# Attention on 64x64 TensorE tiles, with a range of queries for each half of a key tile

## The chip, the core and the metric

One NeuronCore of a Trainium2 chip runs the whole program. The metric is the time of one execution on the device in microseconds (us); lower is better. "Before" and "changed" are the two kernels. TensorE is PE in the profile (PEld: its weight loads), VectorE is DVE, ScalarE is ACT, GpSimd is POOL, SyncE is SP. "Line" numbers such as L274 differ between kernels, because their source lines differ.

## The reference

Sliding-window attention with a few global keys feeds a balanced mixture of experts. Shapes: batch 4, 8 heads, 768 positions, head size 64; 8 global keys, a window of 96.

```python
scores = (q @ k.T) / 8 - slope[h] * dist          # dist = query - key, or 96 for global keys
keep   = (key < 8) | (0 <= query - key < 96)
a      = softmax(where(keep, scores, -1e9))
x      = a @ v                                     # (3072, 512)
logits = x @ w_gate                                # tokens go to 8 experts, 384 each, best first
out[m] = relu(x[m] @ w1[e]) @ w2[e]                # per expert
```

All of attention is done in fp32, because a small error in a logit sends a token to another expert.

## The kernel before

The program has three parts: a loop over 16 pairs of heads (attention), a routing part that is a chain of short steps, and the experts. A key tile has 120 keys and the 8 global ones; it sees 215 queries. Scores have the keys on partitions, so exp (ACT) and the multiplication with a weight table (DVE) act on `P[128 keys, 2 heads, queries]`.

```python
# scores: 64 rows (head t) x 128 columns (keys); the two heads run side by side
nc.tensor.matmul(ps[:, t, o : o + w], lhsT=kA[r, i, :], rhs=qTt[r, KT * i : KT * i + w], ...)
# attend: 128 rows (keys) x 64 columns (head size)
nc.tensor.matmul(po[n][bk][64 * t : 64 * t + 64, ...], lhsT=v7[:, t, i, :], rhs=P[:, t, ...], ...)
# sums: softmax sums and gate logits, 128 rows x 32 columns, four quarters of the queries side by side
nc.tensor.matmul(pr[32 * gq : 32 * gq + 32, ...], lhsT=onesx[:, t, :], rhs=Ps[n, g][:, t, ...], ...)
...
# one pair, in the order of PE (abridged):
# scores 0 | kT of the next pair | attend of the last group before | scores 1 | qT | attend | sums | scores 2 | tok | attend
# POOL issues 1.5 weight pieces (512 KB each in bf16) per pair: 24 pieces for the experts
```

The softmax here doesn't subtract the row's maximum and nothing guards it: scores larger than these inputs give would overflow.

## Time and profile before

Median 342.42 us (342.17 to 342.49, 3 runs). The parts in the table are of the profiled execution, which took 347.1 us.

| part | from the profile |
|---|---|
| loop over pairs | first scores at 10.6 us, logits complete at 174.1 us: 163 us |
| one pair | 10.0 us |
| routing until the first expert matmul | 68 us |
| experts | 103 us |

Each row of the next view, the table of stretches, gives one stretch of 10 us: its length, the busy time of PE, PEld, DVE, ACT and POOL (with counts), the granted clock, the DMA share and GB/s.

```profile
44.00:54.00 10.00, 10.00 (x142) 7.73 (x140) 6.69 (x13) 4.50 (x8) 4.36 (x6) 1.00 1.07 221
84.00:94.00 10.00, 10.00 (x142) 7.73 (x140) 6.70 (x12) 4.51 (x8) 4.35 (x6) 1.00 1.06 205
94.00:104.00 10.00, 10.00 (x142) 7.74 (x140) 8.03 (x13) 4.51 (x8) 3.31 (x5) 1.00 1.10 255
```

PE is never idle from 24 to 154 us; the next busiest engine, DVE, has 6.0 to 8.1 us of every 10. One pair in the timeline of PE (start, length, engine, line, operation, tiles, shape of one, count):

```profile
80.26 0.87 PE L242 MATMUL pt<-ident,kn 128*128 128x128 f32 x6
81.06 0.98 PE L316 MATMUL po<-P,v 128*64 128x215 f32 x12
81.97 1.00 PE L274 MATMUL ps<-qT,kA 64*128 64x215 f32 x8
82.90 0.87 PE L259 MATMUL pt<-ident,qn 128*128 128x128 f32 x6
83.70 0.95 PE L316 MATMUL po<-P,v 128*64 128x215 f32 x8
84.58 1.63 PE L347 MATMUL pr<-P,onesx 128*32 128x192 f32 x45
...
90.27 0.87 PE L242 MATMUL pt<-ident,kn 128*128 128x128 f32 x6
```

The same step comes again after 10.0 us. The shape of the tile (128*128, 128*64, 64*128, 128*32) changes ten times per pair. The second is q8, a DMA queue that the page calls "instruction":

```profile
PE 275.4 (80%) x2820; PEld 188.1 (54%) x2828; DVE 183.3 (53%) x419; ACT 111.4 (32%) x192; POOL 116.7 (34%) x166
...
q8 instruction: 24, 0.39, 0.4%
```

### The profile page before, as it was taken

How to read it: one execution, taken by the hardware profiler on the slowest of the kernel's cores; microseconds unless marked ns; L12 is line 12 of the kernel's file. 1: busy time of each engine (PE TensorE's matmuls, PEld its weight loads, DVE VectorE, ACT ScalarE, POOL GpSimd, SP SyncE). 2: the span in 40 equal slices, each digit the busy share in tenths (PEclk: the TensorE clock that was granted, in tenths of full speed). 3: DMA queues.
4: the chain of work that ended last, by engine and by line, in shares of the span. 5: the costliest groups of instructions: out<-in, count | busy, mean ns of one | idle time of the engine just before them, and what ended most of it. 6: DMA issues, size and time to landing. Idle time of an engine off the chain costs nothing. (4 is left out here: it accounts for less than half of the span.)

```text
span 345.4 us, 7041 instructions
## 1 busy us (share of the span) xinstructions
PE 275.4 (80%) x2820; PEld 188.1 (54%) x2828; DVE 183.3 (53%) x419; ACT 111.4 (32%) x192; POOL 116.7 (34%) x166
## 2 busy tenths in 40 slices
PE   2899999999999999999923222252969999999990
PEld 2577877777777777777712111131525555555540
DVE  5356768676686667765476666691022233222320
ACT  1575444445534444454200000000314422343220
POOL 8553233535323353530210000006753465223321
PEclk9999999999999999999965555555889999999996
DMA  8999999997999979769099900002322332122111
GB/s 149 250 275 219 232 220 229 214 240 197 220 260 190 271 167 215 155 124 180 4 167 227 181 3 0 0 1 63 106 91 77 123 129 84 64 91 93 61 63 67
DMA packets 58359, 49.24 MB, mean 143 GB/s; under 512 B 32976, under 2 KB 51920, under 8 KB 58320
## 3 DMA queue, kind: packets, MB, share of 16 engines
q0 software_dynamic: 15808, 26.22, 37.2%
q1 hardware_dynamic: 42512, 22.50, 26.8%
q8 instruction: 24, 0.39, 0.4%
q14 instruction: 15, 0.12, 0.1%
HBM read 56.05 MB, written 9.44 MB: 190 GB/s over the span
## 5 line engine op out<-in xcount | busy, mean ns | idle before, releaser
L282 ACT ACTIVATE P<-ps 128x860 f32<-128x860 f32 (+1 forms) x48 | 42.7, 889 | 64.3 <-PE ps L274 64.3
L794 ACT ACTIVATE hT<-ph 128x384 bf16<-128x384 f32 x64 | 30.9, 490 | 75.8 <-PE ph L791 70.1
L274 PE MATMUL ps<-qT,kA 64*128 64x215 f32 (+2 forms) x448 | 50.7, 352 | 1.5 <-ACT qT L263 1.5
L774 POOL DMA_INDIRECT xe<-x_tok,idi x24 | 23.0, 958 | 80.1 <-DVE idi L631 60.6
L316 PE MATMUL po<-P,v 128*64 128x215 f32 (+6 forms) x576 | 47.5, 298 | 1.0 <-DVE P L296 1.0
L254 POOL COPY kA<-kA 128x56 f32<-128x56 f32 x16 | 16.3, 1017 | 84.0 <-PE po L316 77.5
L791 PE MATMUL ph<-xT,w_all 128*128 128x384 bf16 x256 | 44.4, 332 | 0.2 <-issue 0.2
L274 PEld LDWEIGHTS ps<-qT,kA 64*128 64x128 f32 x448 | 37.6, 191 | 12.1 <-issue 11.0
L316 PEld LDWEIGHTS po<-P,v 128*64 128x64 f32 x576 | 31.4, 136 | 11.8 <-issue 7.4
L289 DVE TENSOR_TENSOR P<-P,Wm 128x860 f32<-128x860 f32 x16 | 28.5, 1784 | 15.4 <-ACT P L282 15.4
L804 POOL DMA_INDIRECT out_dram<-ot,idi x24 | 23.5, 979 | 37.4 <-DVE ot L803 34.2
L791 PEld LDWEIGHTS <-w_all 128*128 128x128 bf16 x256 | 25.5, 100 | 18.5 <-issue 1.6
L296 DVE TENSOR_TENSOR P<-P,Wm 128x860 f32<-128x860 f32 (+1 forms) x32 | 33.6, 1049 | 2.8 <-ACT P L282 2.8
L781 DVE COPY xT<-pxe 128x512 bf16<-128x512 bf16 x24 | 9.6, 422 | 47.0 <-PE pxe L780 35.5
L803 DVE COPY ot<-po 128x512 f32<-128x512 f32 x24 | 16.6, 692 | 29.9 <-PE po L800 27.8
L800 PEld LDWEIGHTS <-hT 128*128 128x128 bf16 x192 | 18.5, 100 | 24.0 <-ACT hT L794 3.4
L347 PEld LDWEIGHTS pr<-P,onesx 128*32 128x32 f32 x768 | 24.7, 109 | 6.0 <-ACT qT L263 4.4
L347 PE MATMUL pr<-P,onesx 128*32 128x168 f32 (+11 forms) x768 | 27.6, 259 | 0.0
L247 DVE COPY kA<-pt 128x360 f32<-128x360 f32 x32 | 17.0, 533 | 15.8 <-PE pt L242 15.8
L800 PE MATMUL po<-w_early,hT 128*128 128x512 bf16 x92 | 23.2, 401 | 2.8 <-ACT hT L794 2.8
L321 ACT COPY oT<-po 128x384 f32<-128x384 f32 x32 | 15.3, 478 | 20.7 <-PE po L316 20.7
L800 PE MATMUL po<-w_late,hT 128*128 128x512 bf16 x92 | 21.2, 379 | 0.1
(145 smaller groups left out, 308.1 us busy)
## 6 DMA issues: line engine op xcount, KB each, us to landing
w_all<-in_moe_w_dram POOLq DMA_DIRECT2D x16, 512.0 KB
v<-in_v_dram SPq DMA_DIRECT2D x32, 180.0 KB, 4.6
kr<-in_k_dram SPq DMA_DIRECT2D x15, 384.0 KB, 7.0
qr<-in_q_dram SPq DMA_DIRECT2D x15, 384.0 KB, 7.3
w_early<-in_moe_w_dram POOLq DMA_DIRECT2D x8, 512.0 KB
w_late<-in_moe_w_dram POOLq DMA_DIRECT2D x4, 1024.0 KB
x_tok<-x SPq DMA_DIRECT2D x16, 192.0 KB, 3.7
v<-in_v_dram SPq DMA_DIRECT2D x32, 14.0 KB
```

The lines of the kernel that those rows point to most:

```text
L247: nc.vector.tensor_copy(out=kA[:, 0 : NT - 1, 8:128].rearrange("c i (u j) -> c i u j", j=NBLK)[:, :, :, 3 * hf : 3 * hf + 3], in_=pt[:, :, ...
L274: nc.tensor.matmul(ps[:, t, o : o + w], lhsT=kA[r, i, :], rhs=qTt[r, KT * i : KT * i + w], start=True, stop=True)
L282: nc.scalar.activation(P[:, :, 0 : GW[g]], ps[:, :, 0 : GW[g]], AF.Exp, scale=0.125)
L289: nc.vector.tensor_tensor(out=P[:, :, 0:430].rearrange("p t (o w) -> p t o w", o=2), in0=P[:, :, 0:430].rearrange("p t (o w) -> p t o w", ...
L296: nc.vector.tensor_tensor(out=P[:, :, 0 : GW[g]], in0=P[:, :, 0 : GW[g]], in1=Wm[:, h0 : h0 + 2, lo : lo + GW[g]], op=ALU.mult)
L316: nc.tensor.matmul(po[n][bk][64 * t : 64 * t + 64, a - QB * bk : z - QB * bk], lhsT=v7[:, t, i, :], rhs=P[:, t, o + a - q0 : o + z - q0], ...
L347: nc.tensor.matmul(o_, lhsT=l_, rhs=r_, start=first[gq], stop=True, skip_group_check=True)
L774: nc.gpsimd.indirect_dma_start(out=xe, out_offset=None, in_=x_tok[:, :], in_offset=bass.IndirectOffsetOnAxis(ap=idi[:, s : s + 1], axis=0),)
L791: nc.tensor.matmul(ph, lhsT=w1_all[:, e, kc, 128 * fc : 128 * fc + 128], rhs=xT_e[:, kc, :, :].rearrange("p t n -> p (t n)"), start=(kc == ...
L794: nc.scalar.activation(hT[:, fc, :], ph, AF.Relu)
L800: nc.tensor.matmul(po, lhsT=hT[:, fc, 128 * t : 128 * t + 128], rhs=w2_of(e)[:, fc, :], start=(fc == 0), stop=(fc == NFC - 1))
L804: s = nc.gpsimd.indirect_dma_start(out=out[:, :], out_offset=bass.IndirectOffsetOnAxis(ap=idi[:, TSLAB * e + t : TSLAB * e + t + 1], axis= ...
```

## The change

The intent: a half of a key tile (64 keys) sees only 151 or 159 queries, not 215. With 64x64 tiles each half gets its own range, and four tiles work at once: two row groups (halves of the keys, or heads) and two column groups. That cuts the streamed columns by a fifth to a quarter (the prediction has the counts). By choice two row groups never write one output bank at the same time, so attend runs in two phases: row group 0 on bank 0 and 1 on bank 1, then swapped, with an ordering dependency between. There are two score groups per pair in place of three; scores and attend now share one tile shape. The token step comes one pair later, one key eviction moves to ACT, one output copy to DVE, and one weight piece is issued per pair.

```diff
-QW = 215
+QW = 159
...
-            for i in GROUPS[g]:
-                for t in range(2):
-                    nc.tensor.matmul(ps[:, t, o : o + w], lhsT=kA[r, i, :], rhs=qTt[r, KT * i : KT * i + w], ...)
+            for i, q0, o, w in PIECES[g]:
+                for c in range(2):
+                    qa = q0 + (56 * c if i < NT - 1 else 0)
+                    for t in range(2):
+                        nc.tensor.matmul(ps[64 * c : 64 * c + 64, t, o : o + w], lhsT=kA[r, i, 64 * c : 64 * c + 64],
+                                         rhs=qTt[r, qa : qa + w], start=True, stop=True, skip_group_check=True)
...
+            for rg in range(2):                    # attend(n, ph): row groups on two banks in turn
+                bk = rg ^ ph
+                lists.append([(rg, bk) + w for w in windows(rg, QB * bk, QB * bk + QB)])
...
+                            mm = nc.tensor.matmul(po[n][bk][64 * t : 64 * t + 64, ...],
+                                                  lhsT=v7[r, t, i, :], rhs=Ps[n, g][r, t, off : off + z - a], ...)
+                            if ph == 1 and m == 0:
+                                tc.add_manual_dep(mm.ins, between[0].ins.name, SYNC_DEP, ...)
...
+                        nc.tensor.matmul(pr[rg][32 * gq : 32 * gq + 32, a:z], lhsT=l_, rhs=r_, ...)   # sums, 64x32 tiles
```

## The prediction

> **What bounds it.** The attention loop runs from 10.6 us (first scores) to 172 us (last sums); the engine table by stretches shows PE 10.00 us busy of every 10 us from 24 to 154 us, granted clock 1.00, DVE 6.7 to 8.1, ACT 4.5, POOL 3.3 to 4.4. The timeline repeats every 10.0 us per head pair. Routing (172 to 233 us, a DVE/PE latency chain) and experts (233 to 345 us) are untouched. So attention is PE bound.

> **One pair's 10.0 us on PE, from the timeline.** Each fp32 matmul is two records of 0.84 ns per column (215 columns: starts 181 ns apart); tiles of one group run concurrently (starts 7 ns apart). Scores 1291 columns per tile, 2.7 us with weight loads; attend 2.5 us; sums 1.9 us (round-robin over tiles of unequal width: a tile idles about 0.2 us[...]); 18 transposes at 109 ns, 2.0 us. Ten changes of tile shape: about 0.09 us empty each, plus a weight load not hidden (50 to 105 ns). [...](last 191-column record should stream out at 89.25, next shape starts at 89.34).

> **The change.**
> - Columns per tile: scores 1291 to 1002, attend 1291 to about 985, sums 668 to about 540, plus 192 for gates as before.
> - Tile-shape changes: 10 to 4 per pair (scores and attend share 64x64). Weight load of 64 columns is 50 ns where it was 105.
> - More records: 138 to 254 per pair. At 7 ns apart when nothing blocks, issue is no limit, but round-robin blocking stays: attend's second phase pairs 127/151/151 with 159/159/88.
> - Replaying these lists[...]: scores 2.0, attend 2.1, sums 1.7, transposes 2.0, changes 0.4: 8.2 us per pair (the same replay gives 10.1 for before).
> - DVE: masks 2 x 1.2 us for 1.05+1.05+1.85, one key eviction (0.7) to ACT, one oT copy (0.55) from ACT, one more transpose and an add (0.6): about 6.5 us. ACT about 4.4. Neither binds at 8.2.
> - Single score buffer, later token step, order wait of attend's second phase: in my replay all answered early in steady state; the first two pairs (W building on ACT) and the longer drain (attend and sums of pair 15 after the last scores) cost about 4 us over 16 x 8.2.
> - Weight pieces: 1 per pair, not 1.5; six move behind the loop. Queue idle in routing (199 to 233 us) absorbs about 20 us.

> **Critical path.** All PE savings are on it until DVE: 16 x 1.8 = 29 us, less about 6 for fill, drain and the longer Dm building on POOL: 22 us.

> **Prediction: 320 us, range 311 to 332. Faster by over 2%: 0.88; within 2%: 0.08; slower: 0.04.**

> **Right if:** timeline period about 8.2 us; PE still over 95% busy in the loop; last sums near 150 us; routing and experts as long as before; DVE about 80% busy; weights landed before the first gather.

> **Wrong if:** four 64x64 tiles don't stream concurrently at 0.84 ns per column (column starts slower than 181/215 of their width: up to 335 us); short windows are bound by weight loads or by dispatch (sums longer than 1.9 us); chains expo-mask-attend or oT-gates stall PE with the single score buffer (PE idle, released by DVE/ACT); late weights delay experts' gathers; or, better, dispatch blocks less than replayed (7.6 us period, 311 us).

10.0 - 8.2 = 1.8 us per pair, 16 x 1.8 = 29 us, less about 6 us: 22 us off 342 us gives 320 us. The 8.2 us are the estimate; its replay gave 10.1 us for the 10.0 us measured before. What the trace of before shows of its terms: records of 215 columns of one tile start 181 ns apart (86.856 and 87.037 us), and the first ones of two tiles 7 ns apart (86.570 and 86.577). The second records of a group come later than that by 105 ns in scores (weights of 128 columns: 286 ns in place of 181) and by 52 ns in attend (64 columns: 233 ns). At a change of shape PE stood empty for an estimated 0.09 us: the last 191-column record starts at 89.088 us, so at 0.84 ns per column it ends at 89.25, and the first record of the next shape starts at 89.342. In sums one tile stood without a record for about 0.2 us: its last 23-column record started at 84.706 us, its next one (143 columns) at 84.938, 6 ns after the third 192-column record of another tile.

## The result, and the profile after

The changed kernel is slower: median 372.19 us (370.07 to 375.11, 4 runs) against 342.46 us, ratio 1.087 (95% interval 1.079 to 1.096). A ratio here is the mean time of one kernel's fast runs over that of the other's in the same rounds, so it is not quite the ratio of the medians quoted. Executions over 1.5% slower than the fastest of the same kernel are left out of the means. The result is correct. The table is of the profiled executions, 347.1 us before and 375.1 us changed.

| | before | changed | predicted |
|---|---|---|---|
| loop over pairs | 163 us | 193 us | about 140 us |
| routing | 68 us | 69 us | as before |
| experts | 103 us | 100 us | as before |

All of the loss is in the loop. The table of stretches of the changed kernel, with the same columns as before:

```profile
44.00:54.00 10.00, 8.15 (x235) 7.10 (x236) 5.73 (x12) 3.12 (x7) 3.38 (x4) 1.00 0.77 167
84.00:94.00 10.00, 5.84 (x77) 5.38 (x74) 1.96 (x7) 1.60 (x3) 0.00 (x0) 0.66 0.55 93
94.00:104.00 10.00, 10.00 (x300) 9.19 (x300) 7.94 (x16) 5.12 (x9) 4.15 (x5) 1.00 0.64 140
```

PE now idles for part of the time, and every other engine idles more: none took over as the limit. The third stretch is fully busy and holds 300 records, so when PE works it works as fast as hoped. In the timeline of PE, one pair without a stall, from scores to the same scores:

```profile
94.73 1.12 PE L292 MATMUL ps<-qT,kA 64*64 64x159 f32 x32
95.68 1.25 PE L327 MATMUL po<-P,v 64*64 64x7 f32 x36
96.86 1.69 PE L355 MATMUL pr<-P,onesx 64*32 64x151 f32 x85
...
98.91 1.12 PE L292 MATMUL ps<-qT,kA 64*64 64x159 f32 x32
99.85 1.07 PE L327 MATMUL po<-P,v 64*64 64x151 f32 x32
100.85 0.55 PE L389 MATMUL pk<-ident,oT 128*128 128x128 f32 x3
...
102.97 0.50 PE L292 MATMUL ps<-qT,kA 64*64 64x159 f32 x8
```

That pair took 102.97 - 94.73 = 8.24 us; the prediction said 8.2. And here is what happens elsewhere, also in the timeline of PE:

```profile
81.03 0.82 PE L327 MATMUL po<-P,v 64*64 64x88 f32 x15 [1.74 <-issue]
81.79 1.69 PE L355 MATMUL pr<-P,onesx 64*32 64x151 f32 x85
...
83.84 0.62 PE L292 MATMUL ps<-qT,kA 64*64 64x159 f32 x9
88.61 1.33 PE L292 MATMUL ps<-qT,kA 64*64 64x159 f32 x17 [4.16 <-issue]
```

In the middle of one uninterrupted group of scores, after 9 of its records, PE does nothing for 4.16 us. The bracket says "issue": PE waited for nothing that the profile shows. The list of waits (who waits <- for whom: us in total, times, longest) says the same over 25 to 185 us; the sums of the other engines there are consequences.

```profile
ACT P L300 <- PE ps L292: 68.8, 27, 7.7
PEld ps L292 <- issue: 28.7, 39, 4.5
PE ps L292 <- issue: 18.6, 12, 4.2
...
PE po L327 <- issue: 10.8, 10, 2.2
```

Parts 1 and 3 of the page show what grew:

```profile
PE 270.2 (72%) x4684; PEld 201.5 (54%) x4684; DVE 168.5 (45%) x421; ACT 104.4 (28%) x192; POOL 114.9 (31%) x170
...
q8 instruction: 39, 0.64, 0.7%
```

PE has 4684 matmul records and as many weight loads, where it had 2820 and 2828, and queue q8 brought 39 packets of 16,384 bytes instead of 24. Numbering PE's instructions (matmul records, weight loads and its sequencer's own) in the trace in order of time, every idle gap of PE over 0.25 us in the loop but two (1.23 us at 20.05 us, while the loop fills, and 0.79 us at its end) comes at the same place modulo 256. There are 23 of them, 31.8 us in all. This place is called an edge below: one block of 256 ends there and the next begins. The loop has 32 edges, of which 23 show such a gap, and 32 packets of that queue start in it (23.65 to 203.82 us), one after each edge; each is taken here as that of the block that begins at the edge after. Setting the packets beside the edges:

```
changed kernel: edge at     PE passes it  idle before  packet of this block   packet start, from the edge before
  instruction 3009            81.03 us      1.74 us     78.42 to 79.77 us      4.68 us
  instruction 3265            88.61         4.16        86.34 to 87.31         5.30
  instruction 3521            96.13         none        90.24 to 91.40         1.63
  instruction 3777            99.11         none        96.42 to 97.42         0.28
kernel before:
  instruction 2241            94.62         none        87.88 to 88.81         2.94
  instruction 2497           103.52         none        95.34 to 96.73         0.72
```

In the loop of the changed kernel no packet starts before PE has passed the edge ahead of it; it starts 0.2 to 5.3 us later (3.0 us on average), takes about 1 us, and PE, where it waits, starts on the block 1.2 to 1.6 us after the packet landed. That is about 5.5 us on average. From 176 us on, beside weight pieces alone, packets start 3.2 to 4.0 us after the edge; the 5.3 us are beside weights and loads together. The kernel before spends about 9.1 us on a block, and every packet had landed 4.9 us or more before PE began its block. The changed one needs 8.2 us for two blocks, 4.1 us each on average, and idles at 23 of 32 edges.

A second loss goes with the first: the trace shows PE at a granted clock of 0.5 at its longest gaps. In the loop it has seven stretches at half clock, each 3.4 or 6.8 us, 30.7 us together (see the 0.66 above). They lie at the seven longest gaps at edges: one began within the gap of 4.16 us, the other six 0.2 to 1.8 us after gaps of 1.93 to 2.36 us; none lies at the 16 gaps of 0.26 to 1.74 us. As an estimate from these numbers, that costs up to 15 us, part of it counted already as idle.

### The profile page after: what moved, and what is told of

It reads as the page before. It is cut to its first block, busy times and chain, and to the rows that moved or that the text cites. A ratio compares the mean times of both kernels' runs of the same rounds, so it can differ in the third digit from the quotient of the medians.

```text
span 373.3 us, 10787 instructions
## 1 busy us (share of the span) xinstructions
PE 270.2 (72%) x4684; PEld 201.5 (54%) x4684; DVE 168.5 (45%) x421; ACT 104.4 (28%) x192; POOL 114.9 (31%) x170
## 5 line engine op out<-in xcount | busy, mean ns | idle before, releaser
L292 PE MATMUL ps<-qT,kA 64*64 64x159 f32 (+1 forms) x1024 | 43.7, 293 | 23.3 <-issue 18.6
L327 PE MATMUL po<-P,v 64*64 64x151 f32 (+8 forms) x1088 | 49.5, 283 | 14.0 <-issue 13.2
L292 PEld LDWEIGHTS ps<-qT,kA 64*64 64x64 f32 x1024 | 36.7, 141 | 34.7 <-issue 28.9
L300 ACT ACTIVATE P<-ps 128x1002 f32<-128x1002 f32 x32 | 32.3, 1008 | 75.9 <-PE ps L292 75.9
L327 PEld LDWEIGHTS po<-P,v 64*64 64x64 f32 x1088 | 43.0, 145 | 17.1 <-issue 16.0
L306 DVE TENSOR_TENSOR P<-P,Wm 128x1002 f32<-128x1002 f32 x32 | 40.3, 1261 | 2.4 <-ACT P L300 2.4
L396 DVE TENSOR_TENSOR x<-pk,rs 128x384 bf16<-128x384 f32 x32 | 17.6, 557 | 44.7 <-PE pk L389 43.6
L355 PE MATMUL pr<-P,onesx 64*32 64x24 f32 (+18 forms) x1408 | 32.8, 263 | 0.0
L355 PEld LDWEIGHTS pr<-P,onesx 64*32 64x32 f32 x1408 | 29.5, 116 | 2.2
L258 PE MATMUL pt<-ident,kn 128*128 128x128 f32 x96 | 17.4, 302 | 5.2 <-POOL Dm L132 5.2
```

Of the source, the lines that this page charges most:

```text
L258: nc.tensor.transpose(pt[:, jj, :], kn[:, 3 * hf + jj, :, :].rearrange("p t d -> p (t d)"), ident)
L292: nc.tensor.matmul(ps[64 * c : 64 * c + 64, t, o : o + w], lhsT=kA[r, i, 64 * c : 64 * c + 64], rhs=qTt[r, qa : qa + w], start=True, stop= ...
L300: nc.scalar.activation(P, ps[:, :, 0:GW], AF.Exp, scale=0.125)
L306: nc.vector.tensor_tensor(out=P, in0=P, in1=Wm[:, h0 : h0 + 2, QW * g : QW * g + GW], op=ALU.mult)
L327: mm = nc.tensor.matmul(po[n][bk][64 * t : 64 * t + 64, a - QB * bk : z - QB * bk], lhsT=v7[r, t, i, :], rhs=Ps[n, g][r, t, off : off + z ...
L355: nc.tensor.matmul(pr[rg][32 * gq : 32 * gq + 32, a:z], lhsT=l_, rhs=r_, start=first[gq, rg], stop=True, skip_group_check=True)
```

## The experiments

**1. More instructions without the new tiles (e1_split).** The kernel before, with each scores, attend and sums matmul cut in two:

```diff
-                for t in range(2):
-                    nc.tensor.matmul(ps[:, t, o : o + w], lhsT=kA[r, i, :], rhs=qTt[r, KT * i : KT * i + w], ...)
+                for f, l in ((0, w // 2), (w // 2, w)):
+                    for t in range(2):
+                        nc.tensor.matmul(ps[:, t, o + f : o + l], lhsT=kA[r, i, :],
+                                         rhs=qTt[r, KT * i + f : KT * i + l], ...)
+# attend and sums likewise
```

> The kernel before, tile shapes and columns unchanged, with every scores, attend and sums matmul cut into two of half the width: about 516 PE instructions per pair in place of about 276, near the 512 of the changed kernel. Theory I (PE runs out of instructions at the edge of each block of 256, because the next block's 16 KB packet comes late): idle gaps of PE over 0.25 us appear, all at one index modulo 256, 8 to 30 us in total over the loop, and the pair takes 12 to 13 us. Rival R (it is the 64x64 tile shape, its order wait or its single score buffer that stalls PE): no such gaps, the pair takes what the replay of the lists gives, about 11.4 us, and the total is about 342 + 16 x 1.4 = 365 us.

Measured: 381.4 us (one look), loop 202 us, so about 12.4 us per pair (its 38 us over the loop before, spread over 16 pairs of 10.0 us). Gaps at block edges: 10.7 us, all at one index modulo 256 (one other gap of 0.55 us). The timeline of PE shows a matmul of the old 128*64 shape that waits for "issue":

```profile
92.05 0.67 PE L318 MATMUL po<-P,v 128*64 128x72 f32 x15
94.18 1.44 PE L318 MATMUL po<-P,v 128*64 128x36 f32 x17 [1.46 <-issue]
```

So the stall needs no 64x64 tiles; more instructions for the same columns bring it.

**2. The changed program on quiet DMA queues (e2_quiet).** No loads of q, k, v after the first pairs and no weight pieces in the loop; wrong result, PE's loop unchanged.

```diff
-                if n + 4 < NP:
-                    load_qk(n + 4)
...
-                        load_v(n + 2)
...
-                weight_piece()                     # all pieces then come behind the loop
...
-            nc.vector.tensor_copy(out=idi, in_=idf)
+            nc.gpsimd.iota(idi, pattern=[[128, NCHUNK]], base=0, channel_multiplier=1)
```

(One more changed line, not shown, keeps the routing of the wrong values on its usual path.)

> The changed kernel with the loads of q, k, v after the first pairs and the weight pieces taken out of the loop (wrong results on purpose; the row indices of the experts are replaced by a plain count so that they stay in range). The PE program of the loop is the same. Theory I with fetches delayed by other DMA traffic: without traffic the packet of a block starts 0.2 to 0.4 us after the request, as it did in the quiet spots of the changed kernel, so no block edge stalls, the timeline repeats every 8.2 us and the last sums end at 145 to 153 us. Rival R: the period stays near 11.5 us and the last sums near 200 us.

Measured: 333.4 us (one look). The table of stretches, with DMA at 0.02 and 0.01:

```profile
64.00:74.00 10.00, 10.00 (x271) 9.36 (x271) 7.34 (x15) 4.78 (x10) 2.69 (x3) 1.00 0.02 3
74.00:84.00 10.00, 10.00 (x312) 9.16 (x313) 7.75 (x15) 5.38 (x10) 3.91 (x5) 1.00 0.01 3
```

PE is busy throughout both stretches, two blocks take 8.3 us, and the order wait and the single score buffer stall nothing. That ends Rival R. Two details missed. Packets started 0.2 to 1.8 us after an edge, not 0.2 to 0.4. And the last sums ended at 160.2 us (the logits were complete at 162.8), not by 153: three stalls of 0.9 to 1.0 us remained where a finished batch was being stored (packets 2.0 to 2.1 us after the edge), and two of 2.2 and 3.3 us came near the end, when POOL, having run ahead, had already begun the late weight pieces (packets 4.6 and 3.7 us after it).

**3. Only the weight pieces out of the loop (e3_late_weights).** The same removal of `weight_piece()` from the loop, nothing else; correct.

> The changed kernel with only the weight pieces moved behind the loop (right result). Theory I: requests meet q, k, v loads only, wait 1.3 to 2.4 us in place of 3 to 5, so most blocks arrive in time; period 8.2 to 9 us, last sums at 150 to 162 us; the total may still be long, because all 24 pieces then stand in front of the experts' gathers on the same queue: 340 to 385 us. Rival R: last sums near 200 us.

Measured: 342.97 us (one look; the kernel before on the same chip 342.57). The loop fell from 193 to 161 us, gaps at edges from 31.8 to 13.7 us. The last sums ended at 170.8 us (the logits were complete at 173.3), later than the 150 to 162 expected: with q, k, v alone packets still came up to 3.8 us after an edge, and the weight pieces again met the last blocks of the loop. The late weights cost the experts nothing: routing and experts took 68 and 99 us as before.

**4. Weight pieces of a quarter (e4_small_pieces).**

```diff
-                nc.gpsimd.dma_start(dst, s_)
+                for m_ in range(2):
+                    for h_ in range(2):
+                        nc.gpsimd.dma_start(dst[:, m_ * d2 : m_ * d2 + d2, h_ * c : h_ * c + c],
+                                            s_[:, m_ * d2 : m_ * d2 + d2, h_ * c : h_ * c + c])
```

> The changed kernel with each weight piece issued as four DMAs of a quarter. If a fetch waits until the DMA ahead of it in line is done[...], the waits beside weights alone fall from 3.4 us to about 1 us, the gaps at block edges fall by half or more and the kernel takes 335 to 355 us. If it waits for a fixed depth of descriptors or for bandwidth, waits and time stay (368 to 375 us). Rival R: no change.

Measured: 365.99 us (364.7 to 369.6), ratio to before 1.070; gaps at edges 25.5 us. A small gain, far from what was expected; beside weights alone the packet still started 1.8 to 3.4 us after the edge. (In the changed kernel the packets of one whole piece, 512 KB, kept each of the 16 DMA engines busy for 2.8 to 3.8 us on average, in six pieces from 22 to 106 us.) The idea that a fetch waits for one whole DMA in front of it is not supported. What sets its wait stays open.

**5. Fewer instructions for the same columns (f1_merged_late, f2_merged, f3_merged_half).** In sums, the two heads of a window use different columns of the same one-hot matrix, so each needs a matmul. If instead the heads go to different output columns, one matmul of twice the width serves both; DVE then transposes twice as many columns. The three kernels differ only in how many weight pieces are in the loop: none, one per pair, one for every second pair.

```diff
-            pr = [ps_t.tile([128, 192], FP32, ...) for rg in range(2)]
+            pr = [ps_t.tile([128, 2, 192], FP32, ...) for rg in range(2)]
...
-                        for t in range(2):
-                            l.append((a - 192 * gq, z - 192 * gq, onesx[64 * rg : 64 * rg + 64, t, :],
-                                      Ps[n, g][64 * rg : 64 * rg + 64, t, off : off + z - a]))
+                        l.append((a - 192 * gq, z - 192 * gq, onesx[64 * rg : 64 * rg + 64, 0, :],
+                                  Ps[n, g][64 * rg : 64 * rg + 64, :, off : off + z - a]))
...
+            lists[0, 1].append((0, 56, onesx[64:128, 1, :], Ps[n, 0][64:128, :, 0:56]))   # zeros for a corner
```

> The changed kernel with both heads of a sums window in one matmul of twice the columns (22 matmuls in place of 44, one more to fill a corner with zeros, so about 424 PE instructions per pair in place of 512; the transpose after them twice as wide, about 0.7 us of DVE more per pair), and the weight pieces behind the loop. Theory I: a block of 256 now lasts about 5.0 us of PE work, and with q, k, v loads alone a packet is back after 3.7 to 5 us, so nearly no block stalls: period 8.2 to 8.5 us, last sums at 150 to 158 us, 318 to 330 us in all, below the kernel before. If instructions are not the limit (Rival R, or DVE), the loop stays as long as that of the late-weights run, 161 us.

> The changed kernel with the merged sums matmuls alone, one weight piece per pair as in the changed kernel. The same streamed columns, 17% fewer PE instructions. Theory I: with fetches of 5.4 us on average (4 to 7.5) against 5.0 us of work per block, a block takes about 5.8 us, a pair 9.3 to 9.8 us; gaps at block edges 10 to 20 us in place of 31; the loop 165 to 175 us in place of 193 and the kernel 343 to 355 us. Rival R: as slow as the changed kernel or, with more DVE work, slower (370 us or more).

> Merged sums and one weight piece for every second pair, the rest behind the loop. Theory I: between the two others, loop 150 to 165 us, 325 to 342 us in all.

| kernel | weight pieces in the loop | time, median (range) | ratio to before (95%) | loop |
|---|---|---|---|---|
| changed | 1 per pair | 372.19 (370.07 to 375.11) | 1.087 (1.079 to 1.096) | 193 us |
| f2_merged | 1 per pair | 344.27 (343.17 to 346.92, 4 fast runs; two took 350.47 and 353.68) | 1.005 (1.002 to 1.008) | its profile is a slow run |
| f3_merged_half | 1 per 2 pairs | 337.67 (336.22 to 340.4) | 0.987 (0.980 to 0.994) | 158 us |
| f1_merged_late | none | 321.68 (321.25 to 322.68) | 0.940 (0.937 to 0.942) | 141 us |

All three times lie in the ranges that Theory I expected; for f2_merged its loop and gaps stay unchecked, because its only profile is of a slow run (171.5 us, 24.2 us of gaps). Merging alone (changed against f2_merged, fast runs) is worth about 28 us although PE streams nearly the same columns and DVE has more to do. The table of stretches of f1_merged_late:

```profile
84.00:94.00 10.00, 10.00 (x276) 8.55 (x265) 8.88 (x16) 4.12 (x8) 2.87 (x4) 1.00 0.91 210
94.00:104.00 10.00, 9.93 (x265) 8.82 (x258) 7.34 (x17) 5.08 (x8) 2.70 (x3) 1.00 0.72 182
```

PE is full again beside 180 to 210 GB/s of loads. Two scores of the same step start at 85.19 and 93.35 us in its timeline, 8.16 us apart:

```profile
85.19 1.12 PE L291 MATMUL ps<-qT,kA 64*64 64x159 f32 x32
...
93.35 1.12 PE L291 MATMUL ps<-qT,kA 64*64 64x159 f32 x32
```

An unstalled pair of the changed kernel took 8.24 us, so merging hardly shortens the work itself; what it shortens is the list of instructions. Queue q8 brought 33 packets, and the gaps at edges fell to 3.9 us. This version beats both kernels, by 6% and 14% (321.68 against 342.14 and 372.19 us).

**6. Controls (c1_before_late, c2_split_late).** The weight pieces moved behind the loop in the kernel before, and in the split kernel of experiment 1:

```diff
-                weight_piece()
-                if n % 2:
-                    weight_piece()
```

> Control: the kernel before with its weight pieces behind the loop. Its blocks of 256 instructions last 9.2 us and were all back 5 us or more ahead of their use, so Theory I says that quieter DMA queues buy the loop nothing: loop 162 to 164 us, total 340 to 347 us (later weights can only cost). If late weights are a gain by themselves, apart from instructions, it is faster than 338 us, and the gain of the merged, late version is not that of the tiles.

> Control: the split version of the kernel before (516 PE instructions per pair) with its weight pieces behind the loop. Theory I: the loop falls from 201 us to near what the replay gives for its columns alone, 182 to 190 us, and the gaps at block edges to less than half of 10.6 us; 355 to 368 us in all. If its excess of 40 us over the kernel before is only the cost of narrower matmuls, the loop stays near 200 us.

c1_before_late: 345.64 us against 346.71 for the kernel before in the same rounds (a chip on which both ran slower), ratio 0.996 (0.990 to 1.001), loop 164 us. In the trace of the kernel before no gap over 0.25 us lies at an edge in the loop, and quieter queues bought it nothing. c2_split_late: 369.6 us (one look), loop 188 us in place of 202, gaps at edges 2.1 us in place of 10.7. So of the 38 us by which the split kernel's loop exceeds that of before, 14 us went with the weight pieces: 8.6 us of gaps, and up to 3.4 us (an estimate) of the one stretch at half clock, 6.8 us long, which is gone. Of the other 24 us, 2.1 are the gaps that remain; the rest is put down to narrower matmuls, for which the replay of its lists, an estimate, gave 22 us.

## Why the prediction was wrong

- **What bounds the kernel before**: right. PE was busy all the time from 24 to 154 us.
- **Costs of columns, shape changes and transposes**: right in sum. Without a stall a pair takes 8.24 us in the changed kernel and 8.3 us on quiet queues, against 8.2 predicted. In parts (unstalled pair, both groups): scores 1.9 us (2.0 predicted), attend 2.2 (2.1), sums 2.05 with its shape change (1.7 plus 0.1), transposes 2.1 (2.0).
- **Other engines, order wait, single score buffer**: right. On quiet queues DVE is 73 to 78% busy in the two stretches shown, where about 80% was said, and PE waits for none of them in a steady pair.
- **Weights behind the loop**: right in that routing and experts took as long as before. Missed: how late the packets of q8 come beside weights and loads (up to 5.3 us after an edge in the changed kernel, 0.2 to 1.8 us on quiet queues where nothing stalled).
- **The step that failed**: "More records: 138 to 254 per pair. At 7 ns apart when nothing blocks, issue is no limit". The spacing of 7 ns is that of the first records of a group in the trace. Over the loop the changed kernel shows another pace: 5.5 us on average from an edge to the use of the next block, against 4.1 us of work for its 256 instructions. The prediction counted the added instructions, but costed only their starts within a group. The term, zero in the sum, measured 31.8 us idle, and with the half clock after it (up to 15 us, an estimate) it makes up most of the 53 us between the loop as predicted (140 us) and as measured (193 us). The remainder was not taken apart.
- **The list of what would make it wrong** named dispatch, weight loads, chains and late weights, but not queue q8, though part 3 of the page before listed it with 24 packets. In that profile a packet started 1.8 us after the edge on average and took 1.0 us; with the 1.4 us from landing to use that the changed kernel showed, that is an estimate of 4.2 us, with no margin against blocks of 4.1 us.

That the tiles were a sound idea is shown by f1_merged_late, whose pair takes 8.16 us: with fewer instructions and the weights behind the loop the whole program takes 321.68 us, where 320 was predicted for the changed one.

## What to carry to other kernels

When a change adds instructions to PE, compare the time of a block of 256 with the time from an edge to the packet that follows, in the profile of before, at the DMA load that the loop has. Here 254 in place of 138 matmul records per pair turned a gain of 18% per pair (10.0 to 8.2 us) into a loss of 9% of the program. If "issue" idles PE in the middle of a group of matmuls, number its instructions and look at the gaps modulo 256, as was done here. The remedies that worked here were wider matmuls for the same work (372.19 to 344.27 us) and bulk loads moved out of the loop (344.27 to 321.68 us); in the kernel before, with 9.1 us per block, the latter gained nothing (ratio 0.996).
